# One change to a planned attention-and-mixer kernel: who gives a projection's input back, how the first chunk is started, how the last output projection is split, and how long transfers are assumed to take

## The chip, the cores and the metric

The kernel runs on one core of one Trainium2 chip. A core has five engines that run their own instruction streams and wait for each other by semaphores: TensorE (PE, matrix products into eight PSUM banks), VectorE (DVE), ScalarE (ACT), GpSimd (POOL) and SyncE (SP), which here only issues transfers. The metric is the device time of one execution in microseconds. Three runs of the kernel before took 756.38, 755.15 and 756.24 us; the median is 756.24 us.

## The reference

Batch 1, 2048 tokens, width 512, all inputs bfloat16. Two branches read the same `x`, and a gate per token mixes them:

```python
def _A_ref(x, wqkv, wo):                      # 32 heads of 16
    qkv = (x @ wqkv).reshape(B, S, 3, H, Dh).transpose(2, 0, 3, 1, 4)
    q, k, v = qkv[0], qkv[1], qkv[2]
    scores = jnp.einsum("bhqd,bhkd->bhqk", q, k) * (Dh ** -0.5)
    p = _softmax(scores, axis=-1)
    o = jnp.einsum("bhqk,bhkd->bhqd", p, v)
    return o.transpose(0, 2, 1, 3).reshape(B, S, D) @ wo

def _B_ref(x, w1, w2, w3, w4):                # F = 1792
    h = _gelu(_layernorm(x) @ w1)
    hs = shift_quarters(h, (+1, -1, +2, -2)) @ w2   # four feature quarters, shifted in time
    x1 = x + hs
    return x1 + _gelu(_layernorm(x1) @ w3) @ w4

g = _sigmoid((x * gate_w).sum(-1, keepdims=True))
return g * _A_ref(x, wqkv, wo) + (1 - g) * _B_ref(x, w1, w2, w3, w4)
```

(`shift_quarters` stands for four padded slices of `h`.)

## The kernel before, in words

**Attention.** A head has 16 columns, so four heads share the 128 rows of TensorE at a time. The work is cut into 32 rounds of (chunk of 512 queries, group of 8 heads, parity); a round has 64 tiles, each 128 keys by 512 queries of one head, 2048 tiles in all. A tile is one matrix product into a PSUM bank (line 1313, "QK"), an exponential, and products of the exponentials with V (line 1537, "PV"), which add into one bank for the round. The exponential goes one of two ways. On ACT it is exact, two tiles to an instruction of 1024 columns (line 1408). On DVE it is made from bits: one multiply-add into 16-bit integers (line 1439), and then three copies of the tile shifted by constants (line 1482 on DVE, line 1484 on POOL); all four take part in the PV product, so a DVE tile costs four PV products and an ACT tile one.

**The other work.** Projections for q, k and v (lines 964 with 1019, 1046, 1063), the mixer's w1, w2, w3, w4 and the output projection wo are "gens": chains of matrix products into one bank, each cut into four column strips of 32 that run side by side on TensorE. `Gen.take` (line 154) hands out the next product of a strip; the four strips may be at different steps. A gen's input buffer is listed in `frees` of its last product and is given back when that product is done; then the planner may put a new transfer into the same buffer. Layer-normalised rows are written to DRAM and read back transposed into one of two buffers `xnT` (line 1152), four slices of 128 features per chunk of 512 tokens; the w3 gens of chunk 1 and those of chunk 3 use the same buffer.

**What sets the order.** A planner in the kernel file (`Sim`, `pe_pick`) plays the engines forward with assumed durations and writes each engine's instructions in the order that it found. Transfers have assumed lengths (`dma(3100.0, ...)`, in ns). Some forty parameters (`BASE`) steer its choices and are overwritten at stages of eight tiles by the table `STEPS`. On the chip nothing is re-ordered: an instruction late on an in-order engine holds all behind it.

**Start.** The 512 by 512 first chunk of `x` is transposed on TensorE, 16 products (line 996). Feature blocks 0 and 2 go to one bank and 1 and 3 to another; ACT copies the first bank's two blocks out, DVE the second's (line 1006). Then the first q projection (16 products) and the first k projection (16 products of 512 keys) run; DVE turns q into two masked copies (lines 1038 and 1040), ACT casts k (line 1019). The first QK needs both.

**End.** After the last PV the sums of the last round are transposed on DVE (line 1913), inverted, spread (line 1916) and multiplied (line 1926), and a last product with wo (line 1932) closes the four token blocks. Into the same four banks TensorE adds, before that, what of wo is still open (`known`, line 1890: groups 2 and 3, since `LG = 2`) and, for two of the blocks, the mixer's sum by an identity matrix (`add_y`). Groups 0 and 1 were added earlier in gens of their own. `early` lets two of the blocks take their `known` part before the last PV; in the kernel before the condition did not hold.

The rule by which a buffer is handed back, in the kernel before:

```python
o = self.units[k][j]
if min(self.cp) == self.cp[j]:
    for x in self.units[k]:
        if x is not o:
            o.frees += x.frees
            x.frees = []
```

Here `cp[j]` is the step of strip j, already advanced; the slowest strip's product takes over the buffers of the other three, unless those products were done already.

## Time and profile before

| | |
|---|---|
| median of three runs | 756.24 us |
| the profiled execution's own time | 755.0 us |
| its span | 753.0 us |
| busy, of the span | PE 738.9 us, ACT 732.4 us, DVE 685.8 us, POOL 458.2 us |
| first exponential of a tile starts | 10.29 us |
| last exponential of a tile ends | 743.91 us |
| granted TensorE clock | 0.998 |

The span is what the profile covers; the time of the execution is 2.0 us longer. A row of the timeline gives the start, the time that the merged instructions took together, engine, line, what was written from what, the count, and in brackets the idle time just before and what ended it. A row of the groups gives shapes, count, busy time and mean duration of one; durations of neighbours overlap, so busy time over count is the pace and the mean is the latency.

### The profile page before, as it was taken

Reading aid. Unit: us, or ns where it says so; the run is one execution under the profiler, and the core shown is the slowest. Engines: PE = TensorE matmul, PEld = TensorE weight load, DVE = VectorE, ACT = ScalarE, POOL = GpSimd, SP = SyncE. Lnnn points to the kernel's source line nnn. Section 1 sums busy time; section 2 is a strip of 40 time slices with the busy share of each in tenths; the row PEclk is TensorE's granted clock in tenths of the full one; section 3 lists DMA queues with packets and bytes.
Section 4 is the critical chain, followed back from the end, with each engine's and each line's share of the span. In section 5 each row is a group of like instructions: output and inputs, shape, how many; then the busy total and the mean of one; then the engine's idle time right before and its main releaser. Section 6 shows DMA issues by size and latency. Waiting matters only on the chain.

```text
span 753.0 us, 23698 instructions
## 1 busy us (share of the span) xinstructions
PE 738.9 (98%) x9520; PEld 213.2 (28%) x9520; DVE 685.8 (91%) x1422; ACT 732.4 (97%) x768; POOL 458.2 (61%) x456
## 2 busy tenths in 40 slices
PE   8999999999999999998999999999999999999997
PEld 4324322223222222222322222222222223222222
DVE  5999999998999999997999999998989999887897
ACT  6999999999999999998999999999999999999995
POOL 2274686657866676665544545557657877774542
PEclk9999999999999999999999999999999999999999
DMA  9403331221123220025001100012000000101001
GB/s 199 143 4 79 68 85 33 66 66 44 57 61 73 69 55 21 21 72 114 8 24 27 38 26 24 10 30 52 21 20 18 20 6 27 28 24 28 20 7 46
DMA packets 67093, 34.59 MB, mean 46 GB/s; under 512 B 46748, under 2 KB 62380, under 8 KB 66984
## 3 DMA queue, kind: packets, MB, share of 16 engines
q1 hardware_dynamic: 66040, 32.56, 17.0%
q8 instruction: 74, 1.21, 0.7%
q10 hardware_dynamic: 944, 0.52, 0.2%
q14 instruction: 35, 0.29, 0.1%
HBM read 17.40 MB, written 6.81 MB: 32 GB/s over the span
## 4 chain that ended last, share of the span: by engine, by line
PE 85%; DVE 5%; ACT 4%; DMA 4%; issue 1%; POOL 0%; SPq 0%; DVEq 0%; POOLq 0%; ACTq 0%
PE banks L1537 30%; PE banks L1313 29%; PE banks L964 24%; ACT prob L1408 3%; DMA pk<-den 2%; DVE prob L1439 2%; DVE prob L1482 1%; DMA den<-accsb 1%; ACT hT L1218 1%; PE banks L943 0%; DVE st L1122 0%; PE banks L1890 0%; DMA zE_dram<-ot 0%; POOL prob L1484 0%; DMA xnT<-xn_dram 0%
## 5 line engine op out<-in xcount | busy, mean ns | idle before, releaser
L1408 ACT ACTIVATE prob<-banks 128x1024 bf16<-128x1024 f32 (+1 forms) x747 | 687.7, 1143 | 6.3 <-PE banks L1313 5.2
L1484 POOL TENSOR_SCALAR prob<-prob 128x1024 uint16<-128x1024 uint16 x394 | 405.7, 1048 | 255.4 <-DVE prob L1482 108.7
L1439 DVE TENSOR_SCALAR prob<-banks 128x512 uint16<-128x512 f32 x551 | 364.0, 683 | 29.6 <-PE banks L1313 25.6
L1537 PE MATMUL banks<-prob,V 128*17 128x512 bf16 (+1 forms) x3707 | 318.3, 382 | 1.3 <-POOL prob L1484 0.6
L1313 PE MATMUL banks<-q,kT 32*128 32x512 bf16 x2048 | 283.2, 385 | 2.8 <-ACT prob L1408 0.9
L1482 DVE TENSOR_SCALAR prob<-prob 128x1024 uint16<-128x1024 uint16 (+1 forms) x437 | 172.6, 440 | 5.8 <-PE banks L1537 1.7
L1313 PEld LDWEIGHTS <-kT 32*128 32x128 bf16 x2048 | 70.9, 91 | 306.5 <-ACT prob L1408 277.2
L1537 PEld LDWEIGHTS <-V 128*17 128x17 bf16 (+1 forms) x3707 | 71.4, 88 | 122.4 <-issue 102.2
L964 PE MATMUL banks<-xnT,w 128*32 128x512 bf16 x1152 | 91.1, 384 | 3.4 <-DMA xnT<-xn_dram 3.4
L964 PE MATMUL banks<-w,hT 128*32 128x512 bf16 x692 | 63.2, 383 | 0.0
L964 PEld LDWEIGHTS <-w 128*32 128x32 bf16 x1920 | 39.7, 95 | 53.3 <-issue 31.4
L1576 POOL TENSOR_TENSOR oT<-accsb,bcs 128x512 bf16<-128x512 f32 x31 | 39.5, 1275 | 21.0 <-DVE prob L1482 8.4
L964 PE MATMUL banks<-w,hB 128*32 128x512 bf16 x448 | 40.0, 382 | 0.0
L964 PE MATMUL banks<-w,w 128*32 128x256 bf16 (+1 forms) x768 | 38.7, 311 | 0.6 <-DVE V L1063 0.4
L975 PE MATMUL banks<-wo,oD 32*128 32x512 bf16 x72 | 27.7, 384 | 0.0
L1211 DVE CAST hT<-banks 128x512 bf16<-128x512 f32 x28 | 19.1, 682 | 5.2 <-PE banks L964 5.2
L1211 DVE CAST hB<-banks 128x512 bf16<-128x512 f32 x28 | 19.0, 682 | 4.6 <-PE banks L964 4.5
L1558 DVE COPY accsb<-banks 128x512 f32<-128x512 f32 x31 | 21.1, 680 | 1.8 <-PE banks L1537 1.7
L964 PE MATMUL banks<-w,wq 128*32 128x512 bf16 x256 | 21.5, 390 | 0.7 <-ACT w L1006 0.7
L964 PEld LDWEIGHTS <-hT 128*32 128x32 bf16 x692 | 15.9, 95 | 20.3 <-issue 13.7
L1122 DVE BATCH_NORM_STATS2 st<-x_sb 128x6 f32<-128x512 bf16 x32 | 21.1, 678 | 0.0
L964 PE MATMUL banks<-wo,oD 128*32 128x512 bf16 x152 | 20.1, 384 | 0.1
(94 smaller groups left out, 259.1 us busy)
## 6 DMA issues: line engine op xcount, KB each, us to landing
bcs<-rr SPq DMA_DIRECT2D x124, 64.0 KB
xn_dram<-xn SPq DMA_DIRECT2D x32, 128.0 KB
w<-in_B_w_dram SPq DMA_DIRECT2D x5, 512.0 KB
oD<-oT SPq DMA_DIRECT2D x124, 16.0 KB
w<-in_B_w_dram SPq DMA_DIRECT2D x4, 448.0 KB
out_dram<-ot SPq DMA_DIRECT2D x14, 128.0 KB
x_sb<-in_A_x_dram SPq DMA_DIRECT2D x3, 512.0 KB
w<-in_A_wqkv_dram SPq DMA_DIRECT2D x2, 256.0 KB
```

Of the source, the lines that this page charges most:

```text
L964: units.append([Op("col", j, lambda j=j, lf=lf, rf=rf, n0=n0, n1=n1, st=st, sp=sp: nc.tensor.matmul(get()[32 * j:32 * j + 32, n0:n1], lhsT ...
L975: o = Op("row", i, lambda: nc.tensor.matmul(get(), lhsT=lf(0, P)[rows], rhs=rf()[rows], start=False, stop=True, tile_position=(32 * i, 0), ...
L1122: a = dve(600, deps, lambda: nc.vector.bn_stats(out=sb.slot[:], in_=x_sb[:, t, :]), prio=6, at=at, acq=[sb])
L1211: pre.append(evac(g, PSUM_NS, lambda ps, m=m: nc.vector.tensor_copy(out=h2()[:, m, :], in_=ps[:])))
L1313: o = Op("row", i, lambda: nc.tensor.matmul(dst(), lhsT=kT[G][32 * i:32 * i + 32, kt * P:(kt + 1) * P], rhs=qbuf[G, c].slot[32 * i:32 * i ...
L1408: job = act(hold, ops, lambda: nc.scalar.activation(out=prob[:, pb.cut(), :].bitcast(BF16), in_=unit()[:, rb.cut(), :], func=ACT.Exp, scal ...
L1439: return nc.vector.tensor_scalar(out=prob[:, b0.cut() if w == 2 else b0.bufs[h0].slot, :], in0=unit()[:, rb.cut() if w == 2 else rb.bufs[0 ...
L1482: return nc.vector.tensor_scalar(out=cut(k), in0=cut(0), scalar1=float(SHIFT * k), scalar2=None, op0=ALU.add)
L1484: return nc.gpsimd.tensor_scalar(out=cut(k), in0=cut(0 if both else 2), scalar1=1.0, scalar2=float(SHIFT * (k if both else 1)), op0=ALU.mu ...
L1537: return nc.tensor.matmul(one(accs[r])[32 * i:32 * i + n, :], lhsT=lhs(n), rhs=rhs(), start=st and not edge, stop=True, tile_position=(0, ...
L1558: e = dve(PSUM_NS, round_ops[r], lambda: nc.vector.tensor_copy(out=ab.slot[:], in_=one(accs[r])), acq=[ab], prio=0, frees=[accs[r], Call(a ...
L1576: n = gp(1250, d3, lambda: nc.gpsimd.tensor_tensor(out=ob.slot[:], in0=ab.slot[:], in1=bb.slot[:], op=ALU.mult), acq=[ob], frees=[ab, bb], ...
```

## The change

Seven things are changed together.

1. `Gen.take`: a product that carries buffers hands them to a strip that is still behind at the same step, so that they go on to the product of that step that is issued last.
2. First chunk: each of the four feature blocks has a bank of its own (`x_transposes` takes a tuple of blocks); the copies of the second chunk's blocks all go to DVE.
3. `k_first` makes the first 512 keys in two halves of 256 with a bank and an ACT copy each; tiles of the first two key blocks need the first half only. Of the first q copy DVE makes columns 0 to 255 and ACT columns 256 to 511; q's plan waits for two of the four blocks. Second-chunk transposes and v wait until the first half key and the first q copy are done.
4. `LG = 3`: groups 0, 1 and 2 of the last chunk's output projection go into the earlier gens and group 3 alone is left for the end; `add_y` now comes first and starts the sum of its banks; `early` is granted up to 1.5 us after the last PV's time instead of 0.5 us before it.
5. Assumed transfer times are longer (for instance 3000 to 3600 ns for `xnT`, 2000 to 2800 ns for the row sums), and the assumed gelu times differ.
6. `room()` no longer limits other banks before the first tile; two due times and the start of v differ.
7. `STEPS` and `AGE` have new values throughout, so the whole written order is another one.

The diff, with the table cut:

```diff
--- before.py
+++ after.py
@@ -159 @@
         o = self.units[k][j]
-        if min(self.cp) == self.cp[j]:
-            for x in self.units[k]:
-                if x is not o:
-                    o.frees += x.frees
-                    x.frees = []
+        rest = [i for i in range(4) if self.cp[i] < self.cp[j]]
+        if rest:
+            self.units[k][rest[-1]].frees += o.frees
+            o.frees = []
         return o
@@ -481 @@
     COL = True
-    LG = 2
+    LG = 3
 
@@ -527 @@
         MAXU=9,
-        ROT=2, DUE_SH=-14, AT_SH=0, HOLE=7, MAXG=1, CAP2=6, CAP3=0, LIMD=3, RES=0, GATE=2, E_PRIO=2, AFIRST=0, AGE=12000, ROWM=99, ACC2=0, LIMA=3, JOIN=0,
+        ROT=2, DUE_SH=-14, AT_SH=0, HOLE=7, MAXG=1, CAP2=6, CAP3=0, LIMD=3, RES=0, GATE=2, E_PRIO=2, AFIRST=0, AGE=9000, ROWM=99, ACC2=0, LIMA=3, JOIN=0,
     )
@@ -531 @@
     STEPS = {
-        0: dict(P1_PRIO=0.743, PV_IDLE=0.5, LIMD=4, E_PRIO=0.25),
-        1: dict(P1_PRIO=0.414, GP2=0.655, PV_IDLE=0.731, MAXU=7, E_PRIO=2, AGE=20000, ROWM=7),
...
+        0: dict(GP2=0.8, DVE_STOP=13, DVE_ALONE=-158, SL0=60, PRESS=43, DUE_SH=0),
+        1: dict(SL0=130, PRESS=26, MAXU=4, ROT=0),
...
     }
@@ -905 @@
     def load_xT(c, k, part, prio):
-        return dma(3100.0, [], lambda: xT_dma(c, part, k)(nc.sync), hold=1280.0, prio=prio,
+        return dma(3500.0, [], lambda: xT_dma(c, part, k)(nc.sync), hold=1280.0, prio=prio,
                    acq=[wb[f"x{c}{part}"]] if k == 0 else [])
@@ -992 @@
 
-    def x_transposes(c, half, dep):
-        g = gen("t", -1, dep + [j_id], [], due=-9 + half + T1_DUE * c)
-        ks = (half, half + 2)
+    def x_transposes(c, ks, dep):
+        g = gen("t", -1, dep + [j_id], [], due=-9 + ks[0] + T1_DUE * c)
         g.units = [[Op("full", None, lambda k=k, t=t: nc.tensor.transpose(
-            out=one(g.buf).bitcast(BF16)[:, (k // 2) * 512 + t * P:(k // 2) * 512 + (t + 1) * P],
+            out=one(g.buf).bitcast(BF16)[:, ks.index(k) * 512 + t * P:ks.index(k) * 512 + (t + 1) * P],
             in_=x_sb[:, 4 * c + t, k * P:(k + 1) * P], identity=idb[:]), ns=54.0, name="t") for t in range(4)]
@@ -1001 @@
         g.skew = False
-        g.buf.users = 2
-        for k in ks:
-            def cp(k=k):
-                d, s_ = W(f"x{c}0")[:, k, :], one(g.buf).bitcast(BF16)[:, (k // 2) * 512:(k // 2 + 1) * 512]
-                return nc.vector.tensor_copy(out=d, in_=s_) if k % 2 else nc.scalar.copy(out=d, in_=s_)
-            j_xT[c, 0, k] = (dve if k % 2 else act)(340 if k % 2 else 500, g.units[k // 2], cp, prio=0, frees=[g.buf])
+        g.buf.users = len(ks)
+        for n, k in enumerate(ks):
+            on_dve = c or k % 2
+
+            def cp(k=k, n=n, on_dve=on_dve):
+                d, s_ = W(f"x{c}0")[:, k, :], one(g.buf).bitcast(BF16)[:, n * 512:(n + 1) * 512]
+                return nc.vector.tensor_copy(out=d, in_=s_) if on_dve else nc.scalar.copy(out=d, in_=s_)
+            j_xT[c, 0, k] = (dve if on_dve else act)(375 if on_dve else 535, g.units[n], cp, prio=0, frees=[g.buf])
 
@@ -1010 @@
     j_k = {}
+
+    def k_first():
+        for h in range(2):
+            g = gen("k0", -1, [j_xT[0, 0, 0], j_xT[0, 0, 1], dl_w["k0"]],
+                    [(lambda a, b, k=k: W("k")[:, k, a:b],
+                      lambda k=k, h=h: W("x00")[:, k, 256 * h:256 * h + 256], 0, 256, k == 0, k == KT - 1, 107.5)
+                     for k in range(KT)], due=-3 + h)
+            if h:
+                g.ops[-1].frees += [wb["k"], wb["x00"]]
+            j = act(275, g.units[-1], lambda g=g, h=h: nc.scalar.copy(out=kT[0][:, 256 * h:256 * h + 256],
+                                                                      in_=one(g.buf)[:, 0:256]), prio=0, frees=[g.buf])
+            if h:
+                j_k[0, 0] = j
+            else:
+                j_ka.append(j)
+
+    j_ka = []
 
@@ -1016 @@
         g.ops[-1].frees += [wb["k"], wb[f"x{c}0"]]
-        if G == 0 and c == 0:
-            g.due = -3
-            j_k[G, c] = act(500, g.units[-1], lambda: nc.scalar.copy(out=kT[G][:, 0:512], in_=one(g.buf)[:]), prio=0,
-                            frees=[g.buf])
-            return
-        g.due = 14 * c - 6 if G == 0 else g.due
+        g.due = 14 * c - 11 if G == 0 else g.due
         j_k[G, c] = evac(g, PSUM_NS, lambda ps: nc.vector.tensor_copy(out=kT[G][:, c * 512:(c + 1) * 512], in_=ps[:]),
@@ -1030 @@
         part = 1 if c else 0
-        g = gen(f"q{G}", at, [j_xT[c, part, k] for k in range(KT)] + [dl_w["q0" if G == 0 else "q"]],
+        g = gen(f"q{G}", at, [j_xT[c, part, k] for k in range(KT if c or G else 2)] + [dl_w["q0" if G == 0 else "q"]],
                 [(lambda a, b, k=k: wq[:, k, G * P + a:G * P + b],
@@ -1037 @@
 
-            e1 = dve(680, g.units[-1] + [j_m3], lambda: nc.vector.tensor_scalar(
-                out=qb.slot[:, 0, :], in0=one(g.buf)[:], scalar1=mE[:], scalar2=None, op0=ALU.mult), prio=0, acq=[qb])
-            e2 = dve(680, [e1], lambda: nc.vector.tensor_scalar(
-                out=qb.slot[:, 1, :], in0=one(g.buf)[:], scalar1=mO[:], scalar2=None, op0=ALU.mult), prio=0,
+            e1 = [dve(345, g.units[-1] + [j_m3], lambda: nc.vector.tensor_scalar(
+                out=qb.slot[:, 0, 0:256], in0=one(g.buf)[:, 0:256], scalar1=mE[:], scalar2=None, op0=ALU.mult), prio=0,
+                acq=[qb])]
+            e1.append(act(330, g.units[-1] + [j_m3], lambda: nc.scalar.activation(
+                out=qb.slot[:, 0, 256:512], in_=one(g.buf)[:, 256:512], func=ACT.Copy, scale=mE[:]), prio=0))
+            e1[1].need = qb
+            e2 = dve(680, e1, lambda: nc.vector.tensor_scalar(
+                out=qb.slot[:, 1, :], in0=one(g.buf)[:], scalar1=mO[:], scalar2=None, op0=ALU.mult), prio=0.5,
                 frees=[g.buf])
-            j_q[G, c, 0], j_q[G, c, 1] = e1, e2
+            j_q[G, c, 0], j_q[G, c, 1] = sim.add(Job("POOL", 0.0, 0.0, e1, None, prio=0)), e2
             return
@@ -1057 @@
         c = u // 2
-        g = gen("v", at, [j_xT[c, 0, k] for k in range(KT)] + [dl_w[f"v{hh}"]],
+        g = gen("v", at, begun + [j_xT[c, 0, k] for k in range(KT)] + [dl_w[f"v{hh}"]],
                 [(lambda a, b, t=t, k=k: W(f"x{c}0")[:, k, (t % 4) * P + a:(t % 4) * P + b],
@@ -1145 @@
             last.append(g)
-            ds.append(dma(2200.0, [g], lambda t=t, xb=xb: nc.sync.dma_start(
+            ds.append(dma(2600.0, [g], lambda t=t, xb=xb: nc.sync.dma_start(
                 out=xn_dram[which, t * P:(t + 1) * P, :], in_=xb.slot[:]), frees=[xb]))
@@ -1151 @@
         for k in range(KT):
-            js.append(dma(3000.0, ds, hold=1280.0, fn=lambda k=k: nc.sync.dma_start(
+            js.append(dma(3600.0, ds, hold=1280.0, fn=lambda k=k: nc.sync.dma_start(
                 out=tb.slot[:, k, :], in_=xn_dram[which, c * 512:(c + 1) * 512, k * P:(k + 1) * P], transpose=True),
@@ -1180 @@
                     out=hT[:, m, 2 + c * 512:2 + (c + 1) * 512], in_=ps[:])))
-        ge = act(93 + 1700 * KT + 3050, pre, lambda: nc.scalar.activation(
+        ge = act(93 + 1700 * KT + 3450, pre, lambda: nc.scalar.activation(
             out=hT[:, :, 2:2 + S], in_=hT[:, :, 2:2 + S], func=ACT.Gelu_apprx_tanh), prio=0)
@@ -1217 @@
         for n, (c, (_, bb, h2, jx1g)) in enumerate(zip(cs, ups)):
-            ge = act(93 + 427 * FT + (0 if n else 3050), pre, lambda h2=h2: nc.scalar.activation(
+            ge = act(93 + 427 * FT + (0 if n else 2750), pre, lambda h2=h2: nc.scalar.activation(
                 out=h2(), in_=h2(), func=ACT.Gelu_apprx_tanh), prio=-1)
@@ -1307 @@
         c, G, p = rounds[r]
-        return ready_round(r) and j_k.get((G, kt // 4)) is not None and j_k[G, kt // 4].done is not None
+        k = j_ka[0] if G == 0 and kt < 2 else j_k.get((G, kt // 4))
+        return ready_round(r) and k is not None and k.done is not None
 
@@ -1393 @@
     def room():
-        return sim.free["bank"] and others() < K.LIMD
+        return sim.free["bank"] and others() < (K.LIMD if sim.tiles else NBANK)
 
@@ -1561 @@
                  frees=[ab], hold=580.0)
-        d1 = dma(2000.0, [d0], lambda: nc.sync.dma_start(
+        d1 = dma(2800.0, [d0], lambda: nc.sync.dma_start(
             out=kb.slot[:], in_=db.slot[:].rearrange("j (b e) -> (j b) e", e=16)), prio=1, acq=[kb], frees=[db],
@@ -1571 @@
         for j in range(4):
-            d3.append(dma(2200.0, [d2], lambda j=j: nc.sync.dma_start(
+            d3.append(dma(3000.0, [d2], lambda j=j: nc.sync.dma_start(
                 out=bb.slot[32 * j:32 * j + 32, :], in_=rb.slot[j, :].partition_broadcast(32)),
@@ -1610 @@
 
-    x_transposes(0, 0, j_x0)
-    x_transposes(0, 1, j_x0)
-    k_proj(0, 0, -1)
+    for k in range(KT):
+        x_transposes(0, (k,), j_x0)
+    k_first()
     q_proj(0, 0, -1)
-    x_transposes(1, 0, j_x1)
-    x_transposes(1, 1, j_x1)
+    begun = [j_ka[0], j_q[0, 0, 0]]
+    x_transposes(1, (0, 2), j_x1 + begun)
+    x_transposes(1, (1, 3), j_x1 + begun)
     for c in range(1, 4):
@@ -1619 @@
     for u in range(NT // 2):
-        v_proj(u, 0, max(0, P_V[0] * u - P_V[1]))
+        v_proj(u, 0, max(1, P_V[0] * u - P_V[1]))
     for u in range(NT // 2):
@@ -1892 @@
 
-    def known(tt, gs):
+    def known(tt, gs, st=True):
         for G in gs:
-            into(tt, lambda a, b: oDbuf[c, G].slot[:, tt * P + a:tt * P + b], lambda: wo[:, G, :], G == LG, False)
-
-    def add_y(tt):
-        into(tt, lambda a, b: idf[:, a:b], lambda: y_of(tt), False, False)
+            into(tt, lambda a, b: oDbuf[c, G].slot[:, tt * P + a:tt * P + b], lambda: wo[:, G, :], st and G == LG, False)
+
+    def add_y(tt, st):
+        into(tt, lambda a, b: idf[:, a:b], lambda: y_of(tt), st, False)
 
@@ -1903 @@
     tl = min(t for t, _, name, _ in sim.pelog if name == "pv" and t > tl - 250.0)
-    early = (0, 1) if max(d.done for d in packs) < tl - 500.0 else ()
+    early = (0, 1) if max(d.done for d in packs) < tl + 1500.0 else ()
     for tt in early:
@@ -1916 @@
     nc.vector.transpose(out=by32(tr[1]), in_=rdl[:].unsqueeze(2).to_broadcast([P, NT, 32]))
+    for tt in (1, 3):
+        add_y(tt, tt not in early)
     for tt in range(4):
         if tt not in early:
-            known(tt, range(LG, 3))
-    add_y(1)
-    add_y(3)
-    for tt in range(4):
-        if tt not in early:
-            known(tt, (3,))
+            known(tt, range(LG, 4), tt % 2 == 0)
     for h in range(2):
```

386 lines of the change are left out of this document (188 added, 198 removed).

## The prediction

> **What bounds the kernel now.** I read the page's busy line, then the groups by shape, then the timeline of ACT alone, the list of waits, and the stretches that these point to.
>
> ```profile
> span 753.0 us, 23698 instructions
> PE 738.9 (98%) x9520; PEld 213.2 (28%) x9520; DVE 685.8 (91%) x1422; ACT 732.4 (97%) x768; POOL 458.2 (61%) x456
> ```
>
> ```profile
> L1408 ACT ACTIVATE prob<-banks 128x1024 bf16<-128x1024 f32 x746 | 686.5, 1142 | 6.3 <-PE banks L1313 5.2 <-POOL prob L1484 0.7
> L1408 ACT ACTIVATE prob<-banks 128x1536 bf16<-128x1536 f32 x1 | 1.5, 1488 | 0.0
> ```
>
> ```profile
> PEld L1313 <- ACT prob L1408: 277.2, 641, 0.6
> PE banks L964 <- DMA xnT<-xn_dram: 3.4, 2, 2.5
> ```
>
> ```profile
> 10.29 12.02 ACT L1408 ACTIVATE prob<-banks 128x1024 bf16<-128x1024 f32 x13
> 23.09 23.94 ACT L1408 ACTIVATE prob<-banks 128x1024 bf16<-128x1024 f32 x26 [0.78 <-PE banks L1313]
> ...
> 349.79 2.18 ACT L1408 ACTIVATE prob<-banks 128x1024 bf16<-128x1024 f32 x2 [3.37 <-PE banks L1313]
> ...
> 369.44 13.29 ACT L1408 ACTIVATE prob<-banks 128x1024 bf16<-128x1024 f32 x14 [0.67 <-POOL prob L1484]
> ...
> 633.86 110.05 ACT L1408 ACTIVATE prob<-banks 128x1024 bf16<-128x1024 f32 x119
> 748.44 0.69 ACT L1935 ACTIVATE ot<-banks,omg 128x512 bf16<-128x512 f32 x1 [4.53 <-PE banks L1932]
> ```
>
> PE shows more busy time than ACT, but its weight load for QK waited 641 times for an exponential: PE runs just ahead of ACT. ACT works from 10.29 to 743.91 us (633.86 + 110.05) with 6.1 us of gaps between its rows; the three largest are bracketed above, the other four come to 1.3 us. So the span is a sum: 10.29 before the first exponential, 733.62 of ACT (727.5 work and 6.1 gaps), and 9.09 after the last one. I forecast each term.
>
> **Who gives the input back.** The 3.37 us gap is the largest. On PE and SP it looks so:
>
> ```profile
> 345.04 2.43 SPq L1152 DMA_TRANSPOSE xnT<-xn_dram  x2
> ...
> 347.67 0.40 PE L964 MATMUL banks<-xnT,w 128*32 128x512 bf16 x4 [2.48 <-DMA xnT<-xn_dram]
> ...
> 348.94 0.40 PE L964 MATMUL banks<-xnT,w 128*32 128x512 bf16 x4 [0.88 <-DMA xnT<-xn_dram]
> ...
> 349.28 0.39 PE L1313 MATMUL banks<-q,kT 32*128 32x512 bf16 x3
> ```
>
> The written order of the kernel before says why. The two transfers at 345.04 bring chunk 3's rows into the `xnT` buffer of chunk 1, and stand before the last eight products of chunk 1's w3 that read slices 0 and 1: between the transfers these slices are read 52 and then 60 times, not 56 and 56. The strip that carried the buffer ran ahead, its product was done, and the buffer was given away while three strips had yet to read. PE therefore waited 2.48 + 0.88 = 3.36 us for rows of another chunk, and the next QK, at 349.28, stood behind it. In the changed order every slice is read 56 times a chunk, and no w3 product stands behind another chunk's transfer. Value -3.37; ends -3.4 and 0 (another late transfer in its place).
>
> **A long stretch of projections.** The 0.78 us gap has this before it:
>
> ```profile
> 20.53 2.14 PE L964 MATMUL banks<-w,w 128*32 128x512 bf16 x56
> ```
>
> Two prepared exponentials last 2 x 0.920 = 1.84 us (686.5 / 746), less than 2.14. In the changed order the start has at most 32 such products between two QK groups, half of them 256 wide; the longest stretches outside the gelus come, at the pace of this row, to about 2.0 us, near exponentials 82, 546 and 585. Value -0.7; ends -0.8 and +0.5.
>
> **Work on ACT.** The built programs have 746 exponentials of 1024 columns and one of 1536 before, and 749 of 1024 and one of 512 after: ACT takes 1499 tiles instead of 1495 and DVE 549 instead of 553. Three more at 0.920 are 2.76; the wide one goes (-1.4, three tiles at 0.46; its row says at most 1.5); a single one comes (0.46 to 0.69, the 512-column ACT row at 748.44; I take 0.55). Sum +1.9. Gelus, table loads and the gate's exponential stay.
>
> **The start.**
>
> ```profile
> 4.62 1.35 PE L996 MATMUL banks<-idb,x_sb 128*128 128x128 bf16 x16
> 5.56 1.07 ACT L1006 COPY w<-banks 128x512 bf16<-128x512 bf16 x2 [2.26 <-PE banks L996]
> 6.01 0.76 DVE L1006 COPY w<-banks 128x512 bf16<-128x512 bf16 x2 [3.86 <-PE banks L996]
> 6.69 1.05 PE L964 MATMUL banks<-w,wq 128*32 128x512 bf16 x16 [0.72 <-ACT w L1006]
> 7.85 0.75 DVE L1038 TENSOR_SCALAR q<-banks,mE 128x512 bf16<-128x512 f32 x1 [1.09 <-issue]
> 8.65 0.59 ACT L1019 CAST kT<-banks 128x512 bf16<-128x512 f32 x1 [2.02 <-PE banks L964]
> 9.86 0.60 PE L1313 MATMUL banks<-q,kT 32*128 32x512 bf16 x5
> 14.45 0.62 PE L964 MATMUL banks<-w,w 128*32 128x256 bf16 x16
> ```
>
> ```profile
> L1926 DVE TENSOR_TENSOR oT<-banks,accsb 128x256 bf16<-128x256 f32 x2 | 0.8, 419 | 0.0
> ```
>
> ACT's first copy waited for eight transposes (4.62 + 0.68 = 5.30, plus 0.26). With one bank a block it waits for four: 5.22; its second block follows at 5.89 and is out at 6.48; DVE's two are out by 6.43. The q products begin before that, and the last eight, 0.62 us, end at 7.16 instead of 7.74. The half keys, 0.62 each (row at 14.45, overlapped by 0.17), are done at 7.6 and 8.05. DVE's half of q runs 7.27 to 7.69 (0.42, the 256-column row). ACT's half is written to wait for DVE's: 7.75 to 8.21 (estimate from the 0.69 for 512 columns). Key half one follows to about 8.46, half two to 8.7. QK at 8.5 and, with the 0.43 from 9.86 to 10.29, the first exponential at 8.95. Before, the QK also stood behind second-chunk transposes and v. Those now run behind it, where ACT is at its exponentials; the second-chunk copies, 1.07 of ACT, become two more DVE copies, 0.76, while DVE has nothing else due. Value -1.3; ends -0.5 (second-chunk rows or a wait late) and -1.6.
>
> Both q copies before are read by one engine, one after the other (7.85 onward). The Trainium skill, PSUM — Partial Sum Buffer, section "PSUM bank collisions raise a hardware error", says that two engines must not touch the same bank in the same 32 partitions at once, even in other columns, and that software has to order them. By it the split of q buys no overlap; were the halves side by side, ACT's would end at 7.73 and the first exponential start near 8.5, 0.4 earlier than in my sum. No trace here shows such a pair.
>
> **The end.**
>
> ```profile
> 744.33 1.05 PE L1890 MATMUL banks<-wo,oD 128*32 128x512 bf16 x16
> 744.47 0.72 DVE L1913 STREAM_TRANSPOSE accsb<-banks 128x512 f32<-128x512 f32 x1 [0.51 <-PE banks L1537]
> 745.19 1.90 PE L1890 MATMUL banks<-w,idf 128*32 128x512 f32 x16
> 746.52 0.76 DVE L1926 TENSOR_TENSOR oT<-banks,accsb 128x256 bf16<-128x256 f32 x2
> 746.91 1.05 PE L1890 MATMUL banks<-wo,oD 128*32 128x512 bf16 x16
> 747.77 1.05 PE L1932 MATMUL banks<-woL,oT 128*32 128x512 bf16 x16
> ```
>
> oT's first half is there at 746.94, but line 1932 starts at 747.77, behind PE's own additions (744.33 to 747.96). The change takes the first 16 products away and puts 8 of the last 16 before the last PV: 1.90 and 8 products (about 0.5) remain, done 2.5 us after the PV's end at 744.4, when oT is just ready. Value -0.7; ends -0.9 and +0.7. The loss: those 8 products wait for the last oD transfers, and the last PV queues behind them.
>
> ```profile
> 737.73 1.28 POOL L1576 TENSOR_TENSOR oT<-accsb,bcs 128x512 bf16<-128x512 f32 x1
> 739.03 2.97 SPq L1580 DMA_DIRECT2D oD<-oT  x4
> ```
>
> POOL's product began 6.18 us before ACT's end and the transfers were issued by 742.00. In the changed order a POOL shift and a DVE shift stand before it some ten exponentials from the end; I put it at 6.8 us before the end, issue done 2.5 before. Group 2's 16 products move to earlier gens: 4 x 0.22 us of PE, hidden by ACT.
>
> **Costed at nothing.** Longer assumed transfers change no transfer; they move consumers back in the written order, and ACT's tiles cover that. SP has the same number of transfers. PE has seven more turns between QK and the rest, covered by the wait for ACT in the row above; without that cover at most 7 x 0.39 us, a QK group's own time at 349.28. On DVE 28 more shifts arrive and four fewer tiles:
>
> ```profile
> L1439 DVE TENSOR_SCALAR prob<-banks 128x512 uint16<-128x512 f32 x549 | 361.6, 681 | 29.0 <-PE banks L1313 25.1 <-POOL prob L1484 0.3 <-PE banks L1537 0.3
> L1482 DVE TENSOR_SCALAR prob<-prob 128x1024 uint16<-128x1024 uint16 x434 | 172.0, 441 | 5.8 <-PE banks L1537 1.7 <-POOL prob L1484 1.0 <-ACT prob L1408 0.7
> ```
>
> 28 x 0.396 - 4 x 0.66 = +8.4 us, beside ACT; POOL loses 34 shifts.
>
> **Sum.** -3.37 - 0.7 + 1.9 - 1.3 - 0.7 = -4.2 on the span: 748.8, an execution of 750.8 (its 755.0 lay 1.2 below the median). On the median: 756.24 - 4.2 = 752.0 us. The other gaps, 2 us in all, I leave as they are, between 0 and 4.
>
> **Rivals.** First, *the gap moves*: a new order has new late transfers or crowded stretches, and 3.4 us of gaps return. For it: every stage's order is new. Against it: the old gap came from one misplaced transfer. Time 755.4, no measurable change.
>
> Second, slower, *DVE becomes the bound* between the first and second gelu:
>
> ```profile
> 176.60:352.00 175.40, 170.24 (x2099) 46.62 (x2095) 162.16 (x345) 171.51 (x180) 120.16 (x120) 0.99 0.21 55
> 352.00:619.00 267.00, 265.88 (x3360) 71.41 (x3358) 250.86 (x510) 265.86 (x277) 158.27 (x152) 1.00 0.10 26
> 619.00:744.00 125.00, 124.19 (x1586) 36.22 (x1583) 110.20 (x217) 124.83 (x123) 76.19 (x73) 1.00 0.09 23
> ```
>
> ```profile
> 736.66 2.48 DVE L1439 TENSOR_SCALAR prob<-banks 128x512 uint16<-128x512 f32 x4
> ```
>
> These are windows from gelu to gelu; the busy times with their counts are PE, PE's loads, DVE, ACT, POOL. In the first, ACT's 171.51 are 176 exponentials at 0.92 and 9.6 of gelu and loads. The changed order has 191 there (185.3 us), and on DVE 12 more tiles and 25 more shifts: 162.2 + 7.9 + 9.9 = 180, or 97%. The last has 142 exponentials instead of 119 (124.8 + 21.2 = 146), 23 more tiles and 37 more shifts: 110.2 + 15.2 + 14.7 = 140. If DVE cannot pass the 94.0% of its densest window (the second), the two become 191.5 and 149, +6 and +3: 761. No gain is left from 4.2 us on. Against it: the row at 736.66 has four tiles back to back at a pace of 0.60 ((2.48 - 0.68) / 3), not the 0.66 counted, so busy shares overstate.
>
> Third, *the early products wait* for oD until after the last exponential: +0.7 instead of -0.7, 753.4; still faster.
>
> **Chances and range.** Forecast 0.68, third rival 0.10, gap moves 0.12, DVE 0.10. A measurement tells 0.2%, 1.5 us, from no change: faster under 754.7. The first two and a little of the gap rival give faster 0.80, same 0.11, slower 0.09. The range is 749.6 (-0.1 stretch, -0.3 start, -0.2 end, and 1.8 of the other gaps gone) to 756.0, which takes in the gap rival with 0.6 to spare and leaves DVE out.
>
> **What would show it.** Right: no PE wait on `xnT` before the second gelu, first exponential near 9.0, 750 exponentials with gaps of about 2 us, last PV to end under 8.5 us. Wrong: ACT gaps above 5 us, or DVE over 97% with ACT waiting for its banks.

## The result and the profile after

| | before | after |
|---|---|---|
| median of ten runs | 756.54 us | 752.03 us |
| ratio, with its 95% interval | | 0.9934 (0.9914 to 0.9954) |
| the profiled execution and its span | 755.0 and 753.0 us | 750.92 and 749.1 us |
| first exponential starts | 10.29 us | 8.87 us |
| from there to the end of the last exponential | 733.62 us | 731.89 us |
| gaps of ACT in it | 6.1 us | 3.3 us |
| work of ACT in it (the difference) | 727.5 us | 728.6 us |
| from there to the end of the span | 9.09 us | 8.34 us |

The forecast was 752.0 us. The total came out; not all of its terms did. The profile of the kernel after is that of the fastest of its ten executions, and the one before's lies 1.5 us below its median, so the spans differ by 3.9 us and the medians by 4.5. The page and the groups by shape of the kernel after, as they were shown of the kernel before:

```profile
span 749.1 us, 23684 instructions
PE 735.9 (98%) x9516; PEld 211.6 (28%) x9516; DVE 689.9 (92%) x1450; ACT 733.0 (98%) x771; POOL 423.3 (57%) x422
...
L1415 ACT ACTIVATE prob<-banks 128x1024 bf16<-128x1024 f32 x749 | 688.2, 1150 | 1.1 <-PE banks L1320 0.6 <-PE banks L1544 0.2
L1415 ACT ACT_TABLE_LOAD x3 | 3.8, 1283 | 2.8 <-PE banks L1544 2.8
L1415 ACT ACTIVATE prob<-banks 128x512 bf16<-128x512 f32 x1 | 0.7, 724 | 0.0
```

The counts are those of the forecast: 749 and 1, and no row of a wait on `xnT` is left. The table loads, which bring the exponential back after a gelu, now have 2.8 us of idle time ahead of them, and products of V (line 1544) end it. The row of the same group before:

```profile
L1408 ACT ACT_TABLE_LOAD x3 | 3.8, 1283 | 0.1
```

The timeline of ACT in the kernel after shows where these waits lie:

```profile
8.87 37.88 ACT L1415 ACTIVATE prob<-banks 128x1024 bf16<-128x1024 f32 x41 [0.21 <-PE banks L1320]
...
162.12 7.04 ACT L1187 ACTIVATE hT<-hT 128x8192 bf16<-128x8192 bf16 x1
170.54 1.28 ACT L1415 ACT_TABLE_LOAD   x1 [1.38 <-PE banks L1544]
171.83 175.25 ACT L1415 ACTIVATE prob<-banks 128x1024 bf16<-128x1024 f32 x191
...
361.48 1.28 ACT L1415 ACT_TABLE_LOAD   x1 [0.83 <-PE banks L1544]
...
609.60 1.28 ACT L1415 ACT_TABLE_LOAD   x1 [0.56 <-PE banks L1544]
610.89 129.87 ACT L1415 ACTIVATE prob<-banks 128x1024 bf16<-128x1024 f32 x142
```

The gaps of 3.37 and 0.78 us are gone: 41 exponentials run without a break from the start, and 191 between the first two gelus. In their place stand 1.38, 0.83 and 0.56 us at the table loads, 2.77 of the 3.3 us of gaps. The start and the end:

```profile
5.27 1.07 ACT L996 COPY w<-banks 128x512 bf16<-128x512 bf16 x2 [1.97 <-PE banks L984]
...
7.12 0.48 DVE L1040 TENSOR_SCALAR q<-banks,mE 128x256 bf16<-128x256 f32 x1 [0.76 <-PE banks L953]
7.64 0.47 ACT L1043 ACTIVATE q<-banks,mE 128x256 bf16<-128x256 f32 x1 [1.30 <-DVE q L1040]
8.02 0.64 ACT L1010 CAST kT<-banks 128x256 bf16<-128x256 f32 x2
...
8.44 0.39 PE L1320 MATMUL banks<-q,kT 32*128 32x512 bf16 x4 [0.55 <-ACT kT L1010]
```

```profile
740.29 0.81 PE L1898 MATMUL banks<-wo,oD 128*32 128x512 bf16 x7
...
742.57 0.89 PE L1898 MATMUL banks<-wo,oD 128*32 128x512 bf16 x8
...
743.38 0.76 DVE L1931 TENSOR_TENSOR oT<-banks,accsb 128x256 bf16<-128x256 f32 x2
743.86 1.05 PE L1937 MATMUL banks<-woL,oT 128*32 128x512 bf16 x16 [0.40 <-DVE oT L1931]
```

ACT's half of q waits for DVE's, as the forecast had it; the early products do not wait for their transfers (issued by 738.3), and the last product now waits 0.40 us for oT instead of standing behind PE's own additions.

### The profile page after: what moved, and what is told of

Read it like the earlier page. It is cut to its first block, busy times and chain, and to the rows that moved or that the text cites. A ratio compares the mean times of both kernels' runs of the same rounds, so it can differ in the third digit from the quotient of the medians.

```text
span 749.1 us, 23684 instructions
## 1 busy us (share of the span) xinstructions
PE 735.9 (98%) x9516; PEld 211.6 (28%) x9516; DVE 689.9 (92%) x1450; ACT 733.0 (98%) x771; POOL 423.3 (57%) x422
## 4 chain that ended last, share of the span: by engine, by line
PE 86%; ACT 7%; DVE 4%; issue 2%; POOL 0%; DMA 0%; ACTq 0%; DVEq 0%; POOLq 0%
PE banks L1544 30%; PE banks L1320 30%; PE banks L953 25%; ACT prob L1415 6%; DVE prob L1446 1%; DVE prob L1489 1%; PE banks L932 0%; POOL prob L1491 0%; ACT L1415 0%; DVE st L1128 0%; DVE kT L1025 0%; DMA xn_dram<-xn 0%; PE banks L984 0%; DVE hT L1185 0%; DVE xn L1148 0%
## 5 line engine op out<-in xcount | busy, mean ns | idle before, releaser
L1415 ACT ACTIVATE prob<-banks 128x1024 bf16<-128x1024 f32 x750 | 688.7, 1149 | 1.1 <-PE banks L1320 0.6
L1491 POOL TENSOR_SCALAR prob<-prob 128x1024 uint16<-128x1024 uint16 x360 | 370.2, 1045 | 280.5 <-DVE prob L1489 145.5
L1489 DVE TENSOR_SCALAR prob<-prob 128x1024 uint16<-128x1024 uint16 (+1 forms) x465 | 181.2, 434 | 5.3 <-PE banks L1544 2.5
L953 PE MATMUL banks<-xnT,w 128*32 128x512 bf16 x1152 | 98.0, 383 | 0.0
L953 PEld LDWEIGHTS <-w 128*32 128x32 bf16 x1936 | 42.4, 95 | 47.3 <-issue 27.7
L953 PE MATMUL banks<-w,hB 128*32 128x512 bf16 x448 | 37.3, 382 | 0.0
```

Source lines behind the costliest of these rows:

```text
L953: units.append([Op("col", j, lambda j=j, lf=lf, rf=rf, n0=n0, n1=n1, st=st, sp=sp: nc.tensor.matmul(get()[32 * j:32 * j + 32, n0:n1], lhsT ...
L1415: job = act(hold, ops, lambda: nc.scalar.activation(out=prob[:, pb.cut(), :].bitcast(BF16), in_=unit()[:, rb.cut(), :], func=ACT.Exp, scal ...
L1489: return nc.vector.tensor_scalar(out=cut(k), in0=cut(0), scalar1=float(SHIFT * k), scalar2=None, op0=ALU.add)
L1491: return nc.gpsimd.tensor_scalar(out=cut(k), in0=cut(0 if both else 2), scalar1=1.0, scalar2=float(SHIFT * (k if both else 1)), op0=ALU.mu ...
```

## The experiments

Six positions are read from every profile: ACT's first copy, the first exponential, the end of the last one, the sum of ACT's gaps, the work that remains, and the end of the span. They say more than the times, since the times of one kernel lie up to 6 us apart (754.95 to 761.0 in the ten executions of the kernel before). The span is read to 0.1 us, so what is counted to its end is good to 0.05 us. All medians stand beside runs of the kernel before on the same chip.

**The stall alone.** Two entries of the written order change places with the readers; nothing is planned anew.

```diff
+    third = sim.order[sim.mark["xn132"]][0]
+    for k in (0, 1):
+        _, n, fn = sim.order[sim.mark[f"xn13{k}"]]
+        sim.order[sim.mark[f"xn13{k}"]] = (third - 1.0 + 0.1 * k, n, fn)
```

> The kernel before, with nothing changed but the place of two transfers: those of chunk 3's slices 0 and 1 into the xnT buffer of chunk 1 are written just ahead of the third one, that is behind the last of the 56 readers of each slice (before: 52 and 60). Theory (PE stood still for rows of another chunk, given away too early): the ACT gap of 3.37 us near the 380th exponential goes, nothing comes in its place, the other gaps stay near 2.7 us; 3.4 us less than the kernel before, about 753.1 us against 756.5. Rival (the gap moves: something else is late at the same place, or the transfers are late for chunk 3's own products): less than 1 us gained, with a new PE wait for xnT or a new ACT gap within the next 30 us.

750.36 us against 755.57, ratio 0.9925 (0.9912 to 0.9937); the span is 748.7 us, 4.3 less, 0.26 of it by an earlier first copy. (The four late products of each of the two slices now read chunk 1's rows, as they should; in the kernel before they read chunk 3's.) The profile of this kernel, by groups and by ACT's timeline:

```profile
L967 PE MATMUL banks<-xnT,w 128*32 128x512 bf16 x1152 | 91.0, 383 | 0.0
```

```profile
187.28 161.71 ACT L1411 ACTIVATE prob<-banks 128x1024 bf16<-128x1024 f32 x176
349.01 1.28 ACT L1221 ACT_TABLE_LOAD   x1
```

The 176 exponentials between the first two gelus run without a gap; PE's products on `xnT` wait 0.0 us (3.4 before). The gaps went from 6.08 to 2.74 us, by 3.34. The theory of the gap holds, and two transfers in another place give as much as the whole change.

The median fell by 5.2 us, though, and not by 3.4. One thing more changes with the stall: the granted clock of TensorE. In windows with the columns of the prediction (the clock is the third number from the end), first the kernel before, right behind its stall, then this one:

```profile
349.00:352.00 3.00, 3.00 (x28) 0.59 (x27) 1.64 (x3) 2.06 (x3) 0.10 (x1) 0.66 0.46 120
```

```profile
349.00:352.00 3.00, 3.00 (x48) 1.04 (x44) 3.00 (x7) 2.98 (x2) 1.87 (x3) 1.00 0.46 107
```

In all 50 executions of the kernel before beside these experiments the mean granted clock was 0.992 to 0.998; in the 28 of the kernel with the two transfers moved and its variants, 0.998 to 1.000. On three of the four chips the executions of the kernel before at 0.997 or more took 1.0 to 1.7 us less in the mean than those at 0.995 or less; on the fourth they took 0.4 us more. So the stall seems to cost clock as well as its own length; no run separates the two.

**The rule alone, the table alone.** The kernel before with the new `Gen.take` and the old table of parameters; and with the new table and nothing else. Both are planned anew.

> The kernel before with the new rule for handing a buffer on and nothing else of the change; the order is planned anew with the old table of parameters, so it moves everywhere. All slices of xnT are read 56 and 56 times. ACT gets 747 exponentials of 1024 columns, three of 1536 and one of 512: 692.2 us by 0.920, 1.4 and 0.55 against 687.9. Theory (the rule removes the stall, the table has to be fitted to the order again): no PE wait on xnT, -3.4 for the stall, +4.3 of work on ACT, gaps elsewhere between 2 and 6 us: 756 to 761 us. Rival (the rule brings the whole gain by itself): 752 to 753.5 us.

> The kernel before with the new table of planning parameters and nothing else of the change (old rule, old start, old allowances, old end). Here all four slices of chunk 3 are written ahead of the last w3 product of chunk 1 (52 and 60 readers each). ACT gets 751 exponentials of 1024 columns, 691.1 us against 687.9. Theory (the stall comes from the order in which the buffer is handed on, a table fitted to another kernel is worth nothing): PE waits on xnT again for 3 us or more, +3.2 of work, new gaps: 758 to 765 us. Rival (the table is what gains): 752 to 754 us.

With the rule alone 763.38 us, ratio 1.0098 (1.0084 to 1.0112): no wait on `xnT`, but ACT gaps of 10.55 us where I had allowed 6. The largest, on ACT and PE:

```profile
448.66 21.25 ACT L1407 ACTIVATE prob<-banks 128x1024 bf16<-128x1024 f32 x23 [5.40 <-PE banks L1536]
```

```profile
444.29 3.20 PE L963 MATMUL banks<-w,hT 128*32 128x512 bf16 x56
```

The old table lets 56 projections run in one stretch here. The time lies 2.4 us above the expected range. With the table alone 784.95 us, ratio 1.0381 (1.0365 to 1.0396), and 30.2 us of gaps in 27 places. That it would be slow was expected, but not by so much (758 to 765 us), and the reason was another: in all four slices 60 reads come behind the transfer, and yet PE waited 0.9 us on `xnT`, not 3:

```profile
PE banks L954 <- DMA xnT<-xn_dram: 0.9, 2, 0.5
```

So a buffer given back too early does not have to cost much time. Each of the two alone, planned anew, is a loss; no run has the two together without the rest of the change, so that they pay together is not shown, and neither run prices one of them by itself.

**The rest of the change.** The kernel after and the kernel with the two transfers moved, once more, side by side.

> The changed kernel once more, beside the others on one chip. The stall of 3.37 us alone was worth 4.3 us of span (753.0 to 748.7, where 0.26 is an earlier first copy). Theory (the rest of the change adds up to nothing: start -1.1 and end -0.7 against work +1.0 and other gaps +0.65): equal to the kernel before with only the two transfers moved, within 0.7 us, 751 to 752 us. Rival (the rest gains too): at least 1 us faster than that kernel.

> The kernel before with only the two xnT transfers moved behind the last readers, once more, beside the changed kernel on one chip: 750 to 751 us, 4.3 to 5.2 less than the kernel before. Theory: no slower than the changed kernel, to within 0.7 us. Rival: at least 1 us slower than the changed kernel, since start and end of the change are missing.

752.92 and 750.51 us, ratios 0.9969 (0.9954 to 0.9984) and 0.9941 (0.9929 to 0.9954). The theory said within 0.7 us of each other; the changed kernel is 2.4 us the slower one. So the rest of the change cost time. By positions, in the profiles of both kernels and their variants:

| | kernel before, its variants with the same order (6 profiles) | kernel after, its variants with the same order (6) |
|---|---|---|
| ACT's first copy | 5.10 to 5.71 | 5.07 to 5.29 |
| from there to the first exponential | 4.73 to 4.74 | 3.59 to 3.60 (4.16 where TensorE was slow in all 16 transposes, see below; 3.09 and 3.47 with q in one piece) |
| work of ACT after that | 726.3 to 727.5, mean 726.9 | 728.4 to 728.9, mean 728.7 |
| waits at the three table loads | 0 | 2.76 to 2.77 (3 profiles with its own slots) |
| from the last exponential to the end | 9.02 to 9.09 | 8.24 to 8.51 |

In the two profiles taken side by side the first exponential starts 1.78 us earlier in the kernel after (8.66 against 10.44) and the end is 0.74 us shorter. Against that stand 2.42 us more of gaps (5.26 and 2.84; 2.77 are at the table loads, and the 0.78 of the long stretch is gone) and 2.52 more of work (1.8 by the means of the table). The sum is +2.4, the difference of the spans (751.1 and 748.7) and of the medians.

ACT's first copy waits for transposes on TensorE, and these do not always take equally long. The same 16, with no wait before them, in two profiles of one order (the kernel with the two transfers moved):

```profile
4.62 1.09 PE L999 MATMUL banks<-idb,x_sb 128*128 128x128 bf16 x16
```

```profile
4.61 1.82 PE L999 MATMUL banks<-idb,x_sb 128*128 128x128 bf16 x16
```

In the traces they start 0.11 us apart up to some moment and 0.055 us apart behind it. The trace's record of the granted clock begins at that moment, with 1.00: 4.67 us in the first of these two, 6.20 in the second. Profiles in which it falls at about the same time can be compared. At 4.67 us ACT's first copy starts at 5.30 in the old order and at 5.07 in the new one; at 5.2 us, at 5.56 and 5.28; at 6.2 us, at 5.71 and 5.29. So a bank for each block is worth 0.23 to 0.42 us.

**The table loads.** `Run.pick` takes, for the first exponential after each gelu, the slots that came free longest ago; the order is the same.

```diff
+        if self.old:
+            return sorted(free[:self.n])
...
+            if e == "ACT" and self.gelu and isinstance(b, Run):
+                b.old = True
```

> The changed kernel; the first exponential after each gelu takes those prob slots that came free longest ago, not those that came free last. The written order is the same. Theory (the table load after a gelu carries the wait of the next exponential for its prob slot, that is for products of V that ran a moment ago): the gaps of 1.38, 0.83 and 0.56 us at the three table loads go, 2.8 us of ACT idle; what becomes of them is PE's to say, which is 1 to 2 tiles ahead there: 1.5 to 2.8 us less than the changed kernel, 749.2 to 750.5 us. Rival (PE is late at these places itself and the exponential behind the load would wait for its QK instead): the gaps move to the exponentials, less than 0.5 us gained.

751.16 us, 1.8 less than the kernel after beside it. The timeline of ACT in this kernel:

```profile
172.13 1.28 ACT L1422 ACT_TABLE_LOAD   x1
...
362.23 1.28 ACT L1422 ACT_TABLE_LOAD   x1
...
609.79 1.28 ACT L1422 ACT_TABLE_LOAD   x1
611.08 129.91 ACT L1422 ACTIVATE prob<-banks 128x1024 bf16<-128x1024 f32 x142
```

All three gaps are gone, and the exponentials behind them start at once. The table load had carried the wait of the exponential behind it, for products of V that still read its slot, and carried it 1.28 us, the load's own length, earlier than needed. In this profile the transposes were slow and the first exponential starts at 9.45 us instead of 8.66, so the span shows 1.6 us (749.5 against 751.1) of the 2.27 by which the gaps fell. The Trainium skill, ScalarE: Activation LUTs, section "What ACT_TABLE_LOAD costs", puts a switch at 1283 ns for the load and some 1380 ns for a drain. The load agrees (1283). The first gap, 1.38, would look like a drain, but the others were 0.83 and 0.56 and none is left here, where a gelu ends at 609.77 and the load begins at 609.79: here a switch costs the load alone.

**The end.** The kernel with the two transfers moved, and the end in the new form, with 16 products of groups 2 and 3 ahead of the last PV; and the kernel after without its eight early products.

```diff
-    early = (0, 1) if max(d.done for d in packs) < tl - 500.0 else ()
+    early = (0, 1) if max(d.done for d in packs) < tl + 1500.0 else ()
```

```diff
+    early = ()
     for tt in early:
```

> The kernel before with the two xnT transfers moved and the end of the change: the y products first, no split of groups 2 and 3, and the products of groups 2 and 3 of wo for banks 0 and 1 (16 of them) ahead of the last products of V. Behind the last of those are then 16 products of y (1.90 us) and 16 of wo (0.87) instead of 16, 16 and 16. Theory: from the end of the last exponential to the end of the span 8.4 to 8.5 us instead of 9.03, 0.6 less than the kernel with the transfers alone. Rival (the 16 products wait for the last oD transfers, whose issue ended 1.9 us before the last exponential did, and hold up the last products of V): 9.0 to 9.5 us.

> The changed kernel without the eight products of wo ahead of the last products of V: they run behind the products of y instead. From the end of the last exponential to the end of the span the changed kernel took 8.34 and 8.31 us, the kernel before 9.09. With 16 such products ahead the last products of V came 0.8 us later and nothing was gained. Theory (eight products cost about as much ahead as behind; the gain of the end comes from group 2's products going to earlier places): 8.3 to 8.5 us here too. Rival (the early products are what gains): 8.7 us or more.

The first took 9.05 us from the last exponential to the end, no gain against 9.03, and 750.71 us. Neither theory nor rival: PE in this kernel:

```profile
738.80 1.06 PE L1893 MATMUL banks<-wo,oD 128*32 128x512 bf16 x16
...
739.70 0.59 PE L1540 MATMUL banks<-prob,V 128*17 128x512 bf16 x4
```

The products wait for nothing, but their own length puts the last PV, ready when the last exponential ends at 739.05, at 739.70; what is saved behind it is spent ahead of it. The second took 8.24 us where the kernel after has 8.31 and 8.34; its time, 753.41 us, ratio 0.9965 (0.995 to 0.998), is that of the kernel after (0.9969). So the early products gain nothing. By elimination the 0.75 us come from group 2's products, which `LG = 3` moved to earlier gens; no run moves these alone.

**Start.** The kernel after with old slots and q's first copy in one piece on DVE.

```diff
-                out=qb.slot[:, 0, 0:256], in0=one(g.buf)[:, 0:256], scalar1=mE[:], scalar2=None, op0=ALU.mult), prio=0,
+                out=qb.slot[:, 0, :], in0=one(g.buf)[:], scalar1=mE[:], scalar2=None, op0=ALU.mult), prio=0,
...
-            e1.append(act(330, g.units[-1] + [j_m3], lambda: nc.scalar.activation(
-                out=qb.slot[:, 0, 256:512], in_=one(g.buf)[:, 256:512], func=ACT.Copy, scale=mE[:]), prio=0))
+            e1.append(act(330, g.units[-1] + [j_m3], lambda: None, prio=0))
```

> The changed kernel with the old slots after each gelu and with q's first masked copy in one piece of 512 columns on DVE instead of 256 on DVE and then 256 on ACT. Theory (ACT's half waits for DVE's and the first key half waits behind it on ACT): counted from ACT's first copy, the first exponential starts 3.15 to 3.2 us after it instead of 3.60 (5.27 to 8.87, and 5.07 to 8.66); 0.4 us less than the changed kernel with the old slots, 750.3 to 751 us. Rival (the key halves or PE's order set the start): 3.5 us or more.

```profile
7.14 0.75 DVE L1047 TENSOR_SCALAR q<-banks,mE 128x512 bf16<-128x512 f32 x1 [0.72 <-PE banks L960]
7.51 0.81 ACT L1017 CAST kT<-banks 128x256 bf16<-128x256 f32 x2 [1.15 <-PE banks L960]
...
7.94 0.40 PE L1326 MATMUL banks<-q,kT 32*128 32x512 bf16 x4
```

The first exponential starts 3.09 us after the first copy (8.37 after 5.28), 0.5 earlier: one instruction of 512 columns on DVE beats two of 256 that wait for each other. A second profile with q in one piece, that of the four buffers below, has 3.47 us, where the two pieces of the kernel with old slots alone took 4.16; in both of these the transposes were slow to the last. The time does not settle it: 751.48 us against 756.39 on its chip, ratio 0.9935 (0.9916 to 0.9955), where the old slots alone had 0.9952 (0.9936 to 0.9968). What takes time in both is a gap near 90 us, 1.62 us here and 1.53 with the old slots alone. ACT's row of the latter, and DVE's, which name a cause:

```profile
91.06 72.72 ACT L1422 ACTIVATE prob<-banks 128x1024 bf16<-128x1024 f32 x79 [1.53 <-PE banks L1327]
```

```profile
86.93 0.41 DVE L1155 TENSOR_SCALAR xn<-x_sb,rs,nm 128x512 bf16<-128x512 bf16 x1 [1.19 <-DMA xn_dram<-xn]
...
88.22 0.41 DVE L1155 TENSOR_SCALAR xn<-x_sb,rs,nm 128x512 bf16<-128x512 bf16 x1 [0.87 <-DMA xn_dram<-xn]
```

**Transfers that hold up DVE.** Two runs, one for each kernel. In the kernel with the two transfers moved one reciprocal and its product go behind the shifts around them; in the kernel after (with old slots and q in one piece) the normalised rows get four buffers instead of two.

```diff
+    fourth = [i for i in sim.mark["sh"] if i > ra][3]
+    for k, i in enumerate((ra, rb_, rc)):
+        t, n, fn = sim.order[i]
+        sim.order[i] = (max(t, sim.order[fourth][0] + 1.0 + 0.1 * k), n, fn)
```

```diff
+    ring = sim.free["xn"] + sim.free["ot"]
...
+            at = (lambda xb=xb: xb.slot) if which else (lambda t=t: ring[t % 4])
```

> The kernel before with the two xnT transfers moved, and in one round (the fourth denominator, near 116 us) the reciprocal and its product moved on DVE behind the four prob shifts that stand around them, the transfer of the result with them. In three profiles of the kernel without this move DVE waited there for pk 0.85, 1.57 and 2.25 us, and ACT had a gap of 0, 0.76 and 1.44 us at 118 us. Theory (the late transfer holds up DVE, DVE's shifts hold up the products of V, and the next QK stands behind these): no ACT gap between 115 and 121 us whatever pk does; on the median 0.3 to 1 us less than without the move. Rival (DVE's wait is covered, the gap comes from PE's own 16 and 12 products there): the gap stays between 0 and 1.5 us, no gain.

> The changed kernel with the old slots and q in one piece, and the first normalised rows in four buffers instead of two (the two of ot, idle then, serve as well); the written order is the same. In five profiles of the changed kernel and its variants DVE waited for xn buffers 0.8 to 2.7 us between 73 and 89 us, behind xn_dram transfers that SP issues late; ACT had gaps of 0.2 to 2.6 us between 70 and 92 us in the same profiles. Theory (those waits hold up DVE's shifts, and through them the products of V and the next QK): no DVE wait on xn, the gap near 90 us (1.53 and 1.62 us in the two profiles with old slots) goes, the others there go down to 0.5 us in all; 0.7 to 1.5 us less than without it, 750 to 751 us. Rival (the gap near 90 us is PE's own crowd of 28 products): the gap stays above 1 us.

> The kernel before with the two xnT transfers and the one reciprocal moved, once more, beside the best variant of the changed kernel on one chip: 750 to 750.6 us. If the rest of the change has value once its own new waits are gone (start 1.4 earlier, end 0.7 shorter, against 1.6 more work on ACT), the variant is 0.5 us faster than this; if not, this is the faster one.

Without the move, DVE and ACT of the kernel with the two transfers moved (second profile):

```profile
116.68 0.25 DVE L1568 RECIPROCAL pk<-pk 128x16 f32<-128x16 f32 x1 [2.25 <-DMA pk<-den]
```

```profile
119.21 58.79 ACT L1411 ACTIVATE prob<-banks 128x1024 bf16<-128x1024 f32 x64 [1.44 <-PE banks L1316]
```

With it, no gap between 115 and 121 us in two profiles; 750.32 and 750.01 us, ratios 0.9922 (0.9903 to 0.9942) and 0.992 (0.9906 to 0.9934), where the kernel without it had 0.9925 and 0.9941. The median does not tell them apart, and the profiles do not test the theory either. DVE's wait follows the moment at which SP issues the transfer, first without the move, then with it:

```profile
115.12 0.34 SPq L1565 DMA_DIRECT2D pk<-den  x1
```

```profile
111.50 0.35 SPq L1565 DMA_DIRECT2D pk<-den  x1
```

In the two profiles with the move it was issued at 111.50 and 112.97 us, and in those without it at 113.11, 114.64 and 115.12. Of these the first, from the end's experiment, has a DVE wait of 0.85 us and no gap on ACT; the kernel before, with 111.52, has neither. So the gap would likely have been absent in the two without the move as well, and what the move is worth stays open.

The four buffers do more than was expected: 747.91 us, ratio 0.9893 (0.9879 to 0.9906). DVE's rows in this kernel, and ACT's:

```profile
84.91 0.73 DVE L1156 TENSOR_SCALAR ot<-x_sb,rs,nm 128x512 bf16<-128x512 bf16 x2
```

```profile
71.60 1.02 ACT L1423 ACTIVATE prob<-banks 128x1024 bf16<-128x1024 f32 x1 [0.52 <-DVE prob L1497]
73.06 88.14 ACT L1423 ACTIVATE prob<-banks 128x1024 bf16<-128x1024 f32 x96 [0.44 <-PE banks L1328]
```

No wait for `xn` is left (DVE waits once for `ot`, 0.39 us at 51 us), no gap near 90 us, and 1.38 us of gaps in all (3.48 without the buffers). The span fell by 2.2 us, from 749.1 to 746.9; by the ratios it is 3.2 us. Of the six executions without the four buffers three had a granted clock of 0.999 or 1.000 and took 749.94 to 750.93 us, and three had 0.994 to 0.998 and took 752.02 to 752.63; all four with the buffers had 0.999 or 1.000. Against the first three alone the ratios too give 2.2 us. It is the fastest kernel of this study, 2.1 us below the other one beside it (750.01): the start, the end and the new order are worth something once their own waits are gone.

## Why the prediction was right, point by point

- *Who gives the input back, -3.37.* Right in its mechanism. The gap and its wait are gone, and alone it is worth 3.34 us of gaps. In time it is worth more, 4.3 and 5.2 us by the medians of two chips; the clock behind the stall was not in the sum.
- *A long stretch of projections, -0.7.* Right: the gap of 0.78 us is gone, the first 41 exponentials stand without one.
- *Work on ACT, +1.9.* The pair of profiles gave +1.1, but six profiles of each order give +1.8: the term was right and the pair happened to lie close.
- *The start, -1.3.* 1.42 in the pair. Counted from the first copy it is 1.13. I had put 0.34 on a bank for each block (5.22 instead of 5.56), and profiles with an equal pace of TensorE show 0.23 to 0.42. The sum took the 16 transposes to be evenly spaced; they are not, and ACT's first copy moves by up to 0.6 us with their pace (5.10 to 5.71 in the old form). The rule of the Trainium skill that is cited there, that two engines must be kept off one bank, changed nothing here: the halves were written one behind the other, and no run put them side by side.
- *The end, -0.7.* -0.75, but not in the way described: the eight early products are worth nothing, and by elimination it is the other 16 that moved. The third rival (they wait for oD) did not come; with 16 of them, their own length had the same effect.
- *The other gaps, 2 us in all, as they are.* Wrong: 3.3 us in the first profile of the kernel after and 5.3 in the second, of which 2.77 are at the table loads in each. I had only said that a new order might bring new gaps, and looked for them in transfers and projections; which prob slot the first exponential after a gelu takes was in the written order, and I did not look.
- *DVE becomes the bound.* It did not. The window between the first two gelus of the kernel after, with the same columns as before:

```profile
160.80:347.10 186.30, 184.47 (x2252) 49.73 (x2244) 179.59 (x386) 184.87 (x195) 119.14 (x119) 1.00 0.22 58
```

  DVE was busy 179.59 of 186.3 us, 96%, and ACT had no gap among the 191 exponentials; the forecast was 180 and 97%. In the second profile there was one of 0.60 us. In the last window DVE was busy 133 of 145 us, where the forecast was 140.

So the cause of the gain, the stall, was right, and that the total was met, 752.0 against 752.03, is luck. In the first profile the missed gaps (+1.4) nearly met the work that came out low (-0.8) and a start and end that came out a little better. Behind that, two errors offset each other. The forecast put -3.4 on the stall and -0.8 on all the rest. Measured, the removal of the stall alone is worth 4.3 to 5.2 us by the medians, and the rest, beside the kernel without the stall, costs 0.4 us by the spans of the first profiles (749.1 and 748.7) and 2.4 us side by side on one chip, by spans and medians alike. There the same kernel took 752.92 against 754.81.

## What to carry to other kernels

In a kernel whose written order is kept by the hardware, look at what each engine's next instruction waits for, a table load's among them: the wait of the instruction behind it may sit on the load. One misplaced pair of transfers was worth as much as a whole re-planned order, so try the smallest edit of the old order first; the new order was worth some 2 us more only after its slots, its q copy and its buffers were mended.

## What was not expected of the hardware

- The table load after a gelu waited up to 1.38 us for a prob slot that only the next exponential writes; with another slot the wait is 0.
- Behind two waits of PE, 2.48 and 0.88 us, the granted clock was 0.66 over the next 3 us, and the kernel with that stall never had a mean granted clock above 0.998 in 50 executions.
- The same 16 transposes at the start took 1.09 to 1.91 us, and ACT's first copy starts anywhere from 5.10 to 5.71 us with them.
- The same program's early gaps are not the same from one execution to the next. DVE's wait for one and the same `pk` transfer was 0.85, 1.57 and 2.25 us in three profiles of one order up to there, and ACT's gap behind it 0, 0.76 and 1.44 us; the transfer was issued at 113.11, 114.64 and 115.12 us.
- What stays open: that the 1.8 us of extra work on ACT come from the three more exponentials is counted, not tested; what the clock behind the stall costs in time is not separated from the stall; and why SP issues the same transfer up to 2 us later in one execution than in another was not looked into.
